# Padding the k features to full weight loads, masking kv by a factor, and one queue for the first loads, in a fused attention and feed-forward kernel

## The chip, the cores and the metric

The kernel runs on one core of a Trainium2 chip. A core has five engines that run their own instruction streams and wait for each other by semaphores: TensorE (PE, with its weight loads shown apart as PEld), VectorE (DVE), ScalarE (ACT), GpSimd (POOL) and SyncE (SP), which here only issues DMA transfers. ACT and POOL can issue transfers too; each issuing engine has a queue of its own. The metric is the device time of one execution in microseconds. Lower is better.

## The reference

One block on an input of 2048 tokens by 448 features (bf16): a layer norm, then linear attention with 16 heads of 28 features whose feature map is a pair of softmaxes, and beside it a feed-forward part; both are added to the input.

```python
xn = layernorm(x)
# attention
q, k, v = split_heads(xn @ wqkv)                    # 16 heads of 28
pq, pk  = q @ w_phi, k @ w_phi                      # per head, 28 x 28
phi     = lambda p: concat(softmax(p), softmax(-p)) # 56 features per head
kv  = einsum("bhsf,bhsd->bhfd", phi(pk), v)
z   = einsum("bhsf->bhf", phi(pk))
num = einsum("bhqf,bhfd->bhqd", phi(pq), kv)
den = einsum("bhqf,bhf->bhq", phi(pq), z)[..., None] + 1e-6
A   = merge_heads(num / den) @ wo
# feed-forward
B   = silu(xn @ w1) @ w2                            # 448 -> 1792 -> 448
out = x + A + B
```

## The kernel before

Tokens are cut into 16 tiles of 128, each tile a set of rows on the 128 partitions. Nearly every matmul works on 64 contraction rows, and two of them, on the low and the high half of the rows, run side by side.

**Stages.** Each tile is normalised on DVE (`ln_tile`: statistics `bnst`, `bnag`; scale `rstd`; result `xn`). Tiles 0 to 3 are turned over by TensorE (`tr0` to `tr3`) and evicted from PSUM (`ev0` to `ev3`); tiles 4 to 15 are turned over by transposing transfers in SP's queue (`xnT_dma`). The weights of q and k are folded with w_phi in the kernel (`fold_k`, `fold_q`, words f and g of the plan below), from weights that are transposed by transfers (`wT_dma`). The feed-forward's first half is cut into 28 blocks of 256 hidden columns by 512 tokens (words F0 to F27), each evicted by ACT as a silu. v, k and q are made for pairs of tiles (words v, k, q). A k or q block is evicted by ACT as two exponentials, exp(p) and exp(-p), into a tile `Ek_sb` or `Ek_hi`; DVE makes 32 sums and reciprocals; POOL multiplies (`phik` for k in place, `phiq` for q into RA). For q, a transposing transfer in SP's queue (`phqT`) then puts the product into phT.

**kv.** Word K takes two tiles. For each tile, the 896 features (16 heads of 56) are cut into 8 chunks of 112 (two heads). A chunk's features are the weights and two heads' v, with a column of ones, the 58 moving columns; low and high rows go into two PSUM banks, 7 and 6. For the first seven chunks, 128 weight columns are loaded instead of 112: 16 columns of the next chunk go with them, and what they produce is not read. The last chunk has nothing behind it in the tile and loads 112 (`wide`). After the last K, word M (`kvm`) adds the two banks and keeps of each chunk the two diagonal blocks, one per head, by a product with a 0/1 mask: the result is KVm.

**U, W and the rest.** Word U multiplies phT by KVm for a pair of tiles, 8 chunks each; DVE divides (`den`, `rden`, `o`), a transposing transfer in SP's queue turns the result over (`oT_dma`), and word W multiplies it by wo. Words G, Y and E are the second half of the feed-forward; DVE adds the result to x (`out_ev`) and a store follows. A word with a leading a is the first half of its block, with b the second, on the other row halves; "@" names the PSUM banks.

**What sets the order.** Transfers at the start are issued in the order of the code: x tiles 0, 1, 2 to 3, then w1 columns 0 to 511 in two parts (`w1_0`, `w1_0r`) in SP's queue; w1 columns 512 to 1023 (`w1_512`) in ACT's queue, behind a first activation `warm_act`; then the rest of w1, wv, x and others by SP. While these come in, TensorE runs 38 warm-up matmuls. The first three F blocks are then done tile by tile of 128 tokens, in an order written out in a list (00a is block 0, tile 0, first two of three weight row blocks; 00b the third). Chains of names fix the order of the first instructions on DVE and ACT. After that TensorE follows PLAN, a list of 184 words. On the other engines a list scheduler puts the instructions in order, from a model of durations, latencies and transfer rates written in the code; the order of TensorE is fixed by PLAN, and the model's numbers alone change no computation.

**Places.** `kv` (word K), `kvm` (word M), `ek` and `eq` (the k and q feature tiles; q reuses the tiles of `Ek_sb` in a ring of 8), `load`, `load_x` and `load_w1` (first loads), `ones_column` (sets the last feature of each group to one), `phi_q` and `slot` (where tiles of q go in phT: `Ek_hi` and w1 lie in phT's space, so some slots come free with the last K, others with the last F). All matmuls of the program are recorded at one line, L508; ACT's activations at L531; POOL's fills at L538; ordinary loads at L545; transposing transfers at L613.

Of the kernel before, what the change touches and what calls it, by code (L numbers as in the profile page):

```python
# [140 lines left out]
class _Prog:  # L141
# [86 lines left out]
    def schedule(self, stalls=()):  # L228
# [53 lines left out]
        while done < n:  # L282
# [77 lines left out]
          ("pool", "pe"): 100.0}  # L360
PLAN = """r0 aF3@4 r2 r1 bF3 aF6@0 aF4@6 bF6 bF4 aF5@4 av2@2 av0@0 bv2 bF5 av4@6 bv0 bv4 aF10@2 aF9@0 bF10 f0@6 bF9 aF12@4 aF7@2
aF11@0 f1@6 bF11 bF7 bF12 aF25@0 ak2@6 bF25 bk2 av8@4 av12@2 bv8 ak0@0 bv12 bk0 av10@6 aF22@4 bv10 aF17@2 bF22 av14@6
aF14@0 bF17 bv14 aF18@4 bF14 aF27@6 ak4@2 bF27 bF18 bk4 av6@6 ak6@0 ak8@4 bv6 bk8 bk6 ak12@2 aF8@6 bk12 bF8 aY0@45
aF21@0 aY0 aF23@2 bF21 bF23 ak14@6 bY0 g0@1 bk14 bY0 aF13@0 aF19@2 bF13 aF20@4 bF19 aF24@6 bF20 bF24 ak10@0 g1@3 bk10 K0
K6 K4 aq4@2 K12 aq8@4 bq4 K8 K2 s4 aq0@0 bq8 aq6@2 K14 bq0 bq6 bY1@45 K10 M aY1 aq2@2 aF26@0 s6 bq2 bY1 bF26 aG3@23 aY1
aU2@67 s8 aF15@0 bU2 s0 bF15 aF16@4 bG3 bF16 aU4@01 aq12@6 bU4 bq12 aU3@45 bG3 bU3 s2 aG3 aq10@0 aq14@6 bq10 s10 aW2@45
bq14 aG2 aU0@01 bG2 aG4@67 bU0 bW4 bG2 bW2 s12 bG4 aG2 s14 aW3 aG4 aU1@01 bW3 aW4 bU1 bG4 bG5@23 aU5@50 aG6@41 aU6@67
bU5 aG5 bG6 aU7@05 bU6 bG5 bG6 aG5 bU7 aG6 aW0@67 bW5 bW0 aW5 aW6 aW1@05 bW6 bW7@672 bW1 aW7 E14 E15"""


def bass_parallel_sum__linear_kernel_hedgehog__dense_activation_silu__prompt_kernel(
# [36 lines left out]
    with es:  # L408
        def sb(name, shape, dt):
            return es.enter_context(nc.sbuf_tensor(name, shape, dt))  # L410
# [30 lines left out]
        w1_sb = flat[:, 0:4 * FF].rearrange("p (k f) -> p k f", k=4)  # L441
        NEK = 8
        EW = 2 * D
        Ek_sb = sb("Ek_sb", [128, NEK, EW], BF16)
        Ek_hi = flat[:, 4 * FF:4 * FF + NEK * EW].rearrange("p (n c) -> p n c", n=NEK)

# [357 lines left out]
        def proj_block(t, b0, is_k):  # L804
# [3 lines left out]
            def evac():  # L808
                E2 = ek(t, 2)[:, :, 0:2 * D] if is_k else eq(t, 2)
# [60 lines left out]
        def kvm():  # L870
            lo, hi = (banks[KVB - i][0:KP, 0:2 * DA * CC] for i in range(2))
            P.op("act", d_act(464), lambda e: e.activation(kvsum[:], hi, ACTF.Identity), reads=[hi], writes=[kvsum[:]], name="kvhi")
            P.op("dve", d_dve(464), lambda e: e.tensor_tensor(kvsum[:], lo, kvsum[:], ALU.add), reads=[lo, kvsum[:]], writes=[kvsum[:]], name="kvsum")
            src = kvsum[:].rearrange("p (c j e) -> p c j e", c=CC, j=2)
# [205 lines left out]
        for word in PLAN.split():  # L1080
# [159 lines left out]
```

## Time and profile before

| | |
|---|---|
| runs shown, us | 165.96, 148.22, 146.32 (median 148.22) |
| profiled execution, us | 146.37 |
| its span, first to last instruction, us | 145.1 |
| granted TensorE clock, mean | 1.000 |
| busy, share of span | PE 98%, DVE 62%, ACT 55%, POOL 52% |
| DVE's largest groups | sums of k and q features, 24.4 us in 20 instructions |
| POOL's largest groups | products of q features 27.1 us, of k features 26.8 us |
| ACT table loads | 11, 14.1 us |

How to read the profile: times are microseconds unless marked ns. A row of groups reads: line of the code, engine, operation, output tile, input tile, shapes, count, then busy time, mean ns of one, and the idle time of the engine just before them with what ended it. A row of the timeline reads: start, length, engine, line, operation, count. A row of the chain reads: start, length, what. Tiles that share memory are shown under the name of the memory: w1 and the high k tiles as phT, the q features as Ek_sb, normalised tiles and phiq as RA, transposed weights as Y_sb. Matmuls are pipelined, so their ends are modelled; the step from one start to the next is what counts.

### The profile page before, as it was taken

How to read it: one execution, taken by the hardware profiler on the slowest of the kernel's cores; microseconds unless marked ns; L12 is line 12 of the kernel's file. 1: busy time of each engine (PE TensorE's matmuls, PEld its weight loads, DVE VectorE, ACT ScalarE, POOL GpSimd, SP SyncE). 2: the span in 40 equal slices, each digit the busy share in tenths (PEclk: the TensorE clock that was granted, in tenths of full speed). 3: DMA queues.
4: the chain of work that ended last, by engine and by line, in shares of the span. 5: the costliest groups of instructions: out<-in, count | busy, mean ns of one | idle time of the engine just before them, and what ended most of it. 6: DMA issues, size and time to landing. Idle time of an engine off the chain costs nothing.

```text
span 145.1 us, 4509 instructions
## 1 busy us (share of the span) xinstructions
PE 141.6 (98%) x1947; PEld 83.6 (58%) x1947; DVE 89.5 (62%) x195; ACT 79.4 (55%) x96; POOL 75.1 (52%) x93
## 2 busy tenths in 40 slices
PE   7999999999999999999999999999999999999994
PEld 7895444445444544476787655565555555555663
DVE  1969898600760069939049999927796384625822
ACT  4567856479995999979887949228620000000000
POOL 8808567620197008799935999991497600000000
PEclk9999999999999999999999999999999999999999
DMA  4999998746970000000000069959889999633432
GB/s 101 347 346 266 283 153 119 147 87 139 356 203 5 0 2 5 0 0 5 0 5 5 0 88 195 124 108 181 76 164 164 214 193 167 134 74 72 133 127 63
DMA packets 44500, 17.59 MB, mean 121 GB/s; under 512 B 37040, under 2 KB 44096, under 8 KB 44480
## 3 DMA queue, kind: packets, MB, share of 16 engines
q1 hardware_dynamic: 41648, 15.10, 52.7%
q10 hardware_dynamic: 2704, 2.17, 5.3%
q8 instruction: 15, 0.25, 0.8%
q14 instruction: 5, 0.04, 0.1%
q0 software_dynamic: 128, 0.03, 0.1%
HBM read 6.57 MB, written 1.84 MB: 58 GB/s over the span
## 4 chain that ended last, share of the span: by engine, by line
PE 93%; DMA 3%; SPq 1%; DVE 0%; issue 0%
PE psum L508 93%; DMA phT<-in_B_w_dram 3%; SPq L545 1%; PE psum L525 0%; DVE x_sb L988 0%
## 5 line engine op out<-in xcount | busy, mean ns | idle before, releaser
L508 PE MATMUL psum<-xnT,phT 64*128 64x512 bf16 (+1 forms) x428 | 46.9, 350 | 0.3 <-ACT xnT L531 0.2
L508 PE MATMUL psum<-w_sb,hT 64*128 64x448 bf16 (+2 forms) x434 | 46.1, 343 | 0.0
L825 DVE TENSOR_REDUCE Rec<-Ek_sb 128x32 f32<-128x896 bf16 (+1 forms) x20 | 24.4, 1251 | 19.0 <-ACT Ek_sb L531 19.0
L531 ACT ACTIVATE hT<-psum 128x1024 bf16<-128x1024 f32 x28 | 27.7, 1023 | 11.2 <-PE psum L508 11.0
L508 PEld LDWEIGHTS psum<-xnT,phT 64*128 64x128 bf16 (+1 forms) x428 | 22.5, 95 | 18.5 <-ACT vaug L531 0.6
L508 PEld LDWEIGHTS psum<-w_sb,hT 64*128 64x128 bf16 (+1 forms) x434 | 23.2, 94 | 17.2 <-issue 0.2
L861 POOL TENSOR_TENSOR RA<-Ek_sb,Rec 128x896 bf16<-128x896 bf16 x16 | 27.1, 1724 | 6.1 <-DVE Rec L826 5.0
L508 PE MATMUL psum<-Wqk,xnT 64*128 64x432 bf16 x224 | 24.4, 343 | 0.0
L531 ACT ACTIVATE Ek_sb<-psum 128x864 bf16<-128x864 f32 x24 | 20.3, 915 | 5.9 <-PE psum L508 3.7
L835 POOL TENSOR_TENSOR Ek_sb<-Ek_sb,Rec 128x896 bf16<-128x896 bf16 x8 | 13.4, 1699 | 17.7 <-DVE Rec L826 17.6
L508 PEld LDWEIGHTS psum<-Wqk,xnT 64*128 64x128 bf16 x224 | 11.2, 95 | 8.1
L531 ACT ACT_TABLE_LOAD x11 | 14.1, 1283 | 1.7 <-PEq L1225 0.8
L835 POOL TENSOR_TENSOR phT<-phT,Rec 128x896 bf16<-128x896 bf16 x8 | 13.4, 1699 | 1.2 <-issue 0.9
L988 DVE TENSOR_TENSOR x_sb<-psum,x_sb 128x448 bf16<-128x448 f32 (+1 forms) x13 | 7.2, 584 | 9.1 <-PE psum L508 9.1
L508 PE MATMUL psum<-wv,xnT 64*128 64x448 bf16 x112 | 12.2, 349 | 0.0
L690 DVE BATCH_NORM_STATS2 st<-x_sb 128x6 f32<-128x448 bf16 x16 | 9.6, 603 | 2.9 <-DMA x_sb<-in_A_x_dram 2.9
L508 PE MATMUL psum<-wo_sb,vaug 64*128 64x448 bf16 (+1 forms) x102 | 10.7, 338 | 0.0
L705 DVE TENSOR_SCALAR RA<-x_sb,mv,rstd 128x384 bf16<-128x384 bf16 (+4 forms) x29 | 9.0, 348 | 1.6 <-POOL rstd L701 1.5
L967 DVE TENSOR_TENSOR vaug<-psum,rden 128x448 bf16<-128x448 f32 x16 | 9.2, 619 | 0.0
L825 DVE TENSOR_REDUCE Rec<-phT 128x64 f32<-128x1792 bf16 x4 | 8.0, 1990 | 1.9 <-ACT phT L531 1.9
L826 DVE RECIPROCAL Rec<-Rec 128x32 f32<-128x32 f32 (+1 forms) x24 | 8.8, 396 | 0.2
L508 PEld LDWEIGHTS psum<-wv,xnT 64*128 64x128 bf16 x112 | 5.3, 94 | 5.6 <-ACT vaug L531 0.5
(60 smaller groups left out, 109.7 us busy)
## 6 DMA issues: line engine op xcount, KB each, us to landing
out_dram<-x_sb ACTq DMA_DIRECT2D x15, 112.0 KB, 2.4
w_sb<-in_B_w_dram SPq DMA_DIRECT2D x1, 1568.0 KB, 7.9
x_sb<-in_A_x_dram SPq DMA_DIRECT2D x3, 448.0 KB, 6.0
wo_sb<-in_A_wo_dram SPq DMA_DIRECT2D x2, 336.0 KB, 7.5
phT<-in_B_w_dram SPq DMA_DIRECT2D x1, 576.0 KB, 7.0
phT<-in_B_w_dram SPq DMA_DIRECT2D x2, 256.0 KB, 4.4
phT<-in_B_w_dram ACTq DMA_DIRECT2D x1, 384.0 KB, 4.6
wv<-in_A_wqkv_dram SPq DMA_DIRECT2D x1, 336.0 KB, 7.2
```

The costliest lines, as they stand in the source:

```text
L508: r = e.matmul(dst, lhsT, rhs, start=st, stop=sp, skip_group_check=True)
L531: P.op("act", d_act(n), lambda e: e.activation(dst, src, func, scale=scale), reads=[src], writes=[dst], table=table, name=name, **keys)
L545: P.dma(lambda e: e.dma_start(out=dst, in_=src), n / 280.0, writes=[dst], name=name, eng=eng, lat=lat)
L690: P.op("dve", 590, lambda e: e.bn_stats(st6[:, t, :], xs), reads=[xs], writes=[st6[:, t, :]], name=f"bnst{t}", okeys_w=["ln"])
L705: P.op("dve", dur, lambda e: e.tensor_scalar(dst, x_sb[:, t, c0:c1], mv[:, t, 0:1], rstd[:, t:t + 1], ALU.subtract, ALU.mult), reads=[xs, ...
L825: P.op("dve", 50 + 967 * n, lambda e: e.tensor_reduce(R2, E4, AXL.X, ALU.add), reads=[E4], writes=[R2], name="Ssum")
L826: P.op("dve", 135 + 210 * n, lambda e: e.reciprocal(R2, R2), reads=[R2], writes=[R2], name="Rrec")
L835: P.op("pool", 1700, lambda e: e.tensor_tensor(E3, E3, Rk[:, :, None].broadcast_to([128, 32, DH]), ALU.mult), reads=[E3, Rk], writes=[E3], ...
L861: P.op("pool", 1700, lambda e: e.tensor_tensor(dst, Eq, Rq.rearrange("p (c j) -> p c j", c=CC)[:, :, :, None].broadcast_to([128, CC, 4, DH ...
L967: P.op("dve", 620, lambda e: e.tensor_tensor(o3, U3[:, :, 0:DH], rden[:, uq, :, None].broadcast_to([128, H, DH]), ALU.mult), reads=[U3[:, ...
L988: P.op("dve", d_dve(cs.stop - cs.start), lambda e: e.tensor_tensor(res[:, cs], ob, addend[:, cs], ALU.add), reads=[ob, addend[:, cs]], wri ...
```

## The change

Four things are changed. (1) Each k tile gets 16 columns of zeros behind its 896 features (EW = 2*D + 16), filled once by POOL, so that the last chunk loads 128 weight columns too. Ten tiles instead of eight lie in `Ek_sb`, six in `Ek_hi`; the ring of q stays at eight (NEQ). kvsum gives up its own memory and takes that of wv. (2) `kvm` masks by a factor per partition: two ACT copies with a scale, and two DVE instructions that multiply by the factor and add. (3) All first loads go by SP's queue, w1_0 ahead of x tiles 2 and 3, and w1_512 behind w1_0r; blocks 0 and 1 take all three weight row blocks of a tile at once; tile 3's `bnag` goes behind tile 2's `xn` on DVE. (4) PLAN is a new order of the same 184 words, and some numbers of the model differ.

```diff
-PLAN = """r0 aF3@4 r2 r1 bF3 aF6@0 aF4@6 bF6 bF4 aF5@4 av2@2 av0@0 bv2 bF5 av4@6 bv0 bv4 aF10@2 aF9@0 bF10 f0@6 bF9 aF12@4 aF7@2
-aF11@0 f1@6 bF11 bF7 bF12 aF25@0 ak2@6 bF25 bk2 av8@4 av12@2 bv8 ak0@0 bv12 bk0 av10@6 aF22@4 bv10 aF17@2 bF22 av14@6
-aF14@0 bF17 bv14 aF18@4 bF14 aF27@6 ak4@2 bF27 bF18 bk4 av6@6 ak6@0 ak8@4 bv6 bk8 bk6 ak12@2 aF8@6 bk12 bF8 aY0@45
-aF21@0 aY0 aF23@2 bF21 bF23 ak14@6 bY0 g0@1 bk14 bY0 aF13@0 aF19@2 bF13 aF20@4 bF19 aF24@6 bF20 bF24 ak10@0 g1@3 bk10 K0
-K6 K4 aq4@2 K12 aq8@4 bq4 K8 K2 s4 aq0@0 bq8 aq6@2 K14 bq0 bq6 bY1@45 K10 M aY1 aq2@2 aF26@0 s6 bq2 bY1 bF26 aG3@23 aY1
-aU2@67 s8 aF15@0 bU2 s0 bF15 aF16@4 bG3 bF16 aU4@01 aq12@6 bU4 bq12 aU3@45 bG3 bU3 s2 aG3 aq10@0 aq14@6 bq10 s10 aW2@45
-bq14 aG2 aU0@01 bG2 aG4@67 bU0 bW4 bG2 bW2 s12 bG4 aG2 s14 aW3 aG4 aU1@01 bW3 aW4 bU1 bG4 bG5@23 aU5@50 aG6@41 aU6@67
-bU5 aG5 bG6 aU7@05 bU6 bG5 bG6 aG5 bU7 aG6 aW0@67 bW5 bW0 aW5 aW6 aW1@05 bW6 bW7@672 bW1 aW7 E14 E15"""
+PLAN = """r2 aF3@4 r0 r1 bF3 aF4@6 aF6@0 bF4 bF6 aF5@4 av2@2 av0@6 bv2 bF5 bv0 av4@2 aF8@0 bv4 f0@6 aF9@4 bF8 bF9 aF12@2 aF10@6
+f1@0 aF11@4 bF10 bF11 bF12 aF7@0 aF27@6 bF7 ak4@2 av10@4 bF27 av6@0 bv10 bv6 bk4 av8@4 av14@6 ak6@0 bv14 bv8 bk6 aF23@2
+aF21@6 aF20@4 bF23 aF14@0 bF21 bF20 bF14 aF18@2 ak0@6 bF18 bk0 av12@0 ak8@4 bv12 ak10@2 bk8 bk10 ak2@6 aF13@0 bk2 bF13
+bY0@45 aF17@2 bY0 bF17 ak12@6 aY0 g1@1 bk12 aY0 aF26@0 aF16@2 bF26 bF16 aF19@4 aF24@6 bF19 bF24 ak14@0 g0@2 bk14 K0 K10
+K2 K6 aq4@4 aq8@2 bq4 K4 aq6@0 K12 bq6 s4 bq8 aY1@45 K8 aY1 aq0@2 K14 aq2@0 bq0 bY1 M bY1 s6 bq2 aF22@2 aF25@6 bF22 bF25
+aU2@45 aF15@0 bU2 bF15 aG3@23 s8 s0 aq12@6 aq10@0 aU3@45 bq10 bU3 bG3 bG3 bq12 aG2@45 aU4@01 bG2 aq14@6 aG2 aW2 bU4 s2
+bW2 s10 bG2 bq14 s12 aG4@01 aW3 bG4 aU0@56 bW3 aU5@47 bU0 aG3 bW4 bG4 bU5 aU1@62 aG6@53 bU1 aG6 aG4 bG6 bG5@47 aU6@26
+aW4 bG5 bU6 s14 aG5 aU7@01 aG5 bU7 bG6 bW1@26 bW5 aW1 aW5 bW0@01 aW6 aW0 aW7@264 bW6 bW7 E14 E15"""
...
-        NEK = 8
-        EW = 2 * D
+        NEK, NEQ = 10, 8
+        EW = 2 * D + 16
...
-        kvsum = sb("kvsum", [KP, CC * 2 * DA], F32)
+        kvsum = wv[0:KP, 0:4 * DA * CC].bitcast(F32)
...
         load_x(0, 1)
         load_x(1, 2)
+        load(w1_sb[:, 0:2, 0:512], B_w1[0:256, 0:512].rearrange("(k p) f -> p k f", p=128), "w1_0")
         load_x(2, 4)
-        load(w1_sb[:, 0:2, 0:512], B_w1[0:256, 0:512].rearrange("(k p) f -> p k f", p=128), "w1_0")
...
-        load_w1(512, 1024, "act")
+        load_w1(512, 1024)
...
-            def wide(c):
-                return slice(0, 128) if c < CC - 1 else slice(0, KP)
-
...
-            pe_mms([(banks[KVB - i][wide(c), c * 2 * DA:(c + 1) * 2 * DA], ek(t)[r, 0, c * KP:c * KP + wide(c).stop],
+            pe_mms([(banks[KVB - i][:, c * 2 * DA:(c + 1) * 2 * DA], ek(t)[r, 0, c * KP:c * KP + 128],
...
-            P.op("act", d_act(464), lambda e: e.activation(kvsum[:], hi, ACTF.Identity), ...)
-            P.op("dve", d_dve(464), lambda e: e.tensor_tensor(kvsum[:], lo, kvsum[:], ALU.add), ...)
-            P.op("dve", d_dve(464), lambda e: e.tensor_tensor(
-                KVm[0:KP], src, mask2[:, None, :, None].broadcast_to([KP, CC, 2, DA]), ALU.mult), ...)
+            for j in range(2):
+                P.op("act", d_act(232), lambda e, j=j: e.activation(src[:, :, j, :], hi[:, :, j, :], ACTF.Identity, scale=mask2[:, j:j + 1]), ...)
+            for j in range(2):
+                P.op("dve", d_dve(232), lambda e, j=j: e.scalar_tensor_tensor(
+                    KVm[0:KP, :, j, :], lo[:, :, j, :], mask2[:, j:j + 1], src[:, :, j, :], ALU.mult, ALU.add), ...)
...
-        chain("bnst0 bnag0 bnst1 bnag1 rstd0 xn0a xn0 rstd1 xn1 bnst2 bnag2 bnst3 bnag3 rstd2 xn2 rstd3 xn3 ev3".split())
-        chain("warm_act w1_512 ve0 ve1 ev0a ev0 ev1 ve2 ve3 ev2 silu_table".split())
-        byname = {o.name: o for o in P.ops}
-        byname["w1_512"].deps.add(byname["warm_act"].id)
-        byname["w1_512"].odeps -= byname["w1_512"].deps
+        chain("bnst0 bnag0 bnst1 bnag1 rstd0 xn0a xn0 rstd1 xn1 bnst2 bnag2 bnst3 rstd2 xn2 bnag3 rstd3 xn3 ev3".split())
+        chain("warm_act ve0 ve1 ev0a ev0 ev1 ve2 ve3 ev2 silu_table".split())
...
-        for word in "tr0a tr0 tr1 00a 10a 01a 11a 00b 10b 01b 11b tr2 20 21 tr3 02 12 22 03 13 23".split():
+        for word in "tr0a tr0 tr1 00 10 01 11 tr2 20 21 tr3 02 12 22 03 13 23".split():
...
-        chain(["vaug1", "kvm0", "wphi", "wphi1", "wphi2", "wphi3"])
+        memset(Ek_sb[:, :, 2 * D:EW], 0.0, 128, "pad0")
+        memset(Ek_hi[:, :, 2 * D:EW], 0.0, 128, "pad1")
+        chain(["vaug1", "kvm0", "wphi", "wphi1", "wphi2", "wphi3", "pad0", "pad1"])
```

More of the change, by code (lines that the diff above doesn't have):

```diff
@@ L441, in bass_parallel_sum__linear_kernel_hedgehog__dense_activation_silu__prompt_kernel @@
         w1_sb = flat[:, 0:4 * FF].rearrange("p (k f) -> p k f", k=4)
-        NEK = 8
-        EW = 2 * D
+        NEK, NEQ = 10, 8
+        EW = 2 * D + 16
         Ek_sb = sb("Ek_sb", [128, NEK, EW], BF16)
-        Ek_hi = flat[:, 4 * FF:4 * FF + NEK * EW].rearrange("p (n c) -> p n c", n=NEK)
+        Ek_hi = flat[:, 4 * FF:4 * FF + (NT - NEK) * EW].rearrange("p (n c) -> p n c", n=NT - NEK)
         def ek(t, w=1):
@@ L538, in memset, with load @@
             P.op(eng, d_pool(n, 0.5), lambda e: e.memset(dst, v), writes=[dst], name=name)
-        def load(dst, src, name, eng="sp", lat=1700.0):
+        def load(dst, src, name, eng="sp", lat=1900.0):
             n = 2
@@ L544, in load @@
                 n *= cnt
-            P.dma(lambda e: e.dma_start(out=dst, in_=src), n / 280.0, writes=[dst], name=name, eng=eng, lat=lat)
+            P.dma(lambda e: e.dma_start(out=dst, in_=src), n / 290.0, writes=[dst], name=name, eng=eng, lat=lat)
         memset(ones_bf[:], 1.0, 128, "ones")
@@ L580, in load_x @@
         def load_x(t0, t1):
-            load(x_sb[:, t0:t1, :], rows_of(A_x, t0, t1), f"x{t0}", lat=1400.0)
+            load(x_sb[:, t0:t1, :], rows_of(A_x, t0, t1), f"x{t0}", lat=1250.0 if t0 < 2 else 1500.0)
         def load_rows4(dst, src, c0, c1, name, eng="sp"):
@@ L790, in eq @@
         def eq(t, w=1):
-            n = q_order.index(t) % NEK
+            n = q_order.index(t) % NEQ
             return Ek_sb[:, n:n + w, :]
@@ L808, in evac @@
             def evac():
-                E2 = ek(t, 2)[:, :, 0:2 * D] if is_k else eq(t, 2)
+                E2 = ek(t, 2)[:, :, 0:2 * D] if is_k else eq(t, 2)[:, :, 0:2 * D]
                 src = psum[:, b0 * 512:(b0 + 2) * 512].rearrange("p (i c) -> p i c", i=2)[:, :, 0:DQ].rearrange("p i (h f) -> p i h f", f=DF)
@@ L840, in kv @@
         def kv(ts):
-            def wide(c):
-                return slice(0, 128) if c < CC - 1 else slice(0, KP)
             P.cur_slack = 250.0
-            pe_mms([(banks[KVB - i][wide(c), c * 2 * DA:(c + 1) * 2 * DA], ek(t)[r, 0, c * KP:c * KP + wide(c).stop],
+            pe_mms([(banks[KVB - i][:, c * 2 * DA:(c + 1) * 2 * DA], ek(t)[r, 0, c * KP:c * KP + 128],
                      vaug[r, t, 2 * c:2 * c + 2, :].rearrange("p h c -> p (h c)"),
                      t == 0 and c == 0, t == NT - 1) for t in ts for c in range(CC) for i, r in enumerate((LOW, HIGH))],
-                   "kv_mm", dur=CC * 31.2 * len(ts), keys_w=["kvbank"], mode=64)
+                   "kv_mm", dur=CC * 28.7 * len(ts), keys_w=["kvbank"], mode=64)
             P.cur_slack = 0.0
@@ L857, in phi_q @@
             sp = n % NPQ
-            Eq = eq(t)[:, 0, :].rearrange("p (c j f) -> p c j f", c=CC, f=DH)
+            Eq = eq(t)[:, 0, 0:2 * D].rearrange("p (c j f) -> p c j f", c=CC, f=DH)
             dst = phq[:, sp, :, 0:KP].rearrange("p c (j f) -> p c j f", f=DH)
@@ L870, in kvm @@
         def kvm():
[L871 to L874, printed above, removed]
-            P.op("dve", d_dve(464), lambda e: e.tensor_tensor(
-                KVm[0:KP], src, mask2[:, None, :, None].broadcast_to([KP, CC, 2, DA]), ALU.mult),
-                reads=[src, mask2[:]], writes=[KVm[0:KP]], name="kvm")
+            lo, hi = (banks[KVB - i][0:KP, 0:2 * DA * CC].rearrange("p (c j e) -> p c j e", c=CC, j=2) for i in range(2))
+            src = kvsum.rearrange("p (c j e) -> p c j e", c=CC, j=2)
+            for j in range(2):
+                P.op("act", d_act(232), lambda e, j=j: e.activation(src[:, :, j, :], hi[:, :, j, :], ACTF.Identity, scale=mask2[:, j:j + 1]),
+                     reads=[hi, mask2[:]], writes=[src[:, :, j, :]], name="kvhi")
+            for j in range(2):
+                P.op("dve", d_dve(232), lambda e, j=j: e.scalar_tensor_tensor(
+                    KVm[0:KP, :, j, :], lo[:, :, j, :], mask2[:, j:j + 1], src[:, :, j, :], ALU.mult, ALU.add),
+                    reads=[lo, src, mask2[:]], writes=[KVm[0:KP, :, j, :]], name="kvm")
         early = {int(w[2]) for w in PLAN.split() if w[1:2] == "Y"}
@@ L1124, in bass_parallel_sum__linear_kernel_hedgehog__dense_activation_silu__prompt_kernel @@
                 kv(range(t0, t0 + 2))
-                if t0 < NEK:
+                if t0 < NEQ:
                     ones_column(t0, t0 + 2)
```

## The prediction

> **What bounds the kernel now.** I read the page first, then the chain of work that ended last, then TensorE's own timeline, because all three turn out to say the same thing. From the page:
>
> ```profile
> span 145.1 us, 4509 instructions
> ...
> PE 141.6 (98%) x1947; PEld 83.6 (58%) x1947; DVE 89.5 (62%) x195; ACT 79.4 (55%) x96; POOL 75.1 (52%) x93
> ...
> PEclk9999999999999999999999999999999999999999
> ```
>
> TensorE is busy for 98% of the span and its granted clock is full in every slice. The chain, in order of time, shows where the other 2% lies:
>
> ```profile
> 2.68 5.04 DMA phT<-in_B_w_dram
> ...
> 9.50 30.98 PE psum L508 x345
> ...
> 40.48 102.59 PE psum L508 x1503
> ...
> 143.10 0.39 DVE x_sb L988
> ```
>
> Two unbroken runs of matmuls hold 9.50 to 143.07 us. Ahead of them stands one transfer of w1; behind them one DVE addition and the last store. A busy TensorE can hide slow matmuls, so I compared matmul starts in the timeline: blocks of 64-row matmuls of 512, 448 and 432 columns start every 108, 94.5 and 91.2 ns, 0.211 ns a column in all three. They scale with their columns alone, so no fixed cost is left in them. By that rate 16 matmuls of 58 columns would take 196 ns; over it lie 0.05 us in each kv tile and 0.03 in each U tile, and in all the rest a few stops of 0.05 to 0.2 us. A change of order alone can therefore gain a few tenths at most after 11.44 us; it can lose much more.
>
> **Part 1: kv weight loads.** For each of 16 tiles, kv issues 16 matmuls of 58 columns; 14 load 128 weight columns, the two of the last chunk only 112. Two groups by form (last columns: busy us, mean ns, idle before):
>
> ```profile
> L508 PEld LDWEIGHTS psum<-vaug,Ek_sb 64*128 64x128 bf16 x112 | 2.2, 97 | 0.1
> ...
> L508 PEld LDWEIGHTS psum<-vaug,Ek_sb 64*112 64x112 bf16 x16 | 1.1, 127 | 0.0
> ```
>
> The narrower load is the longer one. What that costs is read from TensorE's timeline (start, us, count), where the same 58-column matmul also occurs with 128-column loads only, in U:
>
> ```profile
> 72.58 1.67 PE L508 MATMUL psum<-vaug,Ek_sb 64*128 64x58 bf16 x96
> 74.08 0.72 PE L508 MATMUL psum<-Wqk,xnT 64*128 64x432 bf16 x6
> ```
>
> ```profile
> 121.75 0.62 PE L508 MATMUL psum<-KVm,phT 64*128 64x58 bf16 x32
> 122.20 2.81 PE L508 MATMUL psum<-w_sb,hT 64*128 64x448 bf16 x28
> ```
>
> From start to next start, 96 kv matmuls take 1.50 us (250 ns a tile) and 32 U matmuls 0.45 (225 to 229 ns a tile). 16 tiles by 22 ns are **0.36 us off TensorE**, on the path, since no other engine releases these blocks later than TensorE reaches them. Bounds: 0 (a load is hidden by something else) to 0.40 (225 ns everywhere). The 16 padding columns cost two POOL fills behind the four small loads of w_phi; POOL is idle there from 6.73 to 10.61 us waiting for those loads, and a 128x128 fill took 0.2 us: nothing, and 0.4 us of BD's start if that cover went.
>
> The Trainium skill, "TensorE: Matmul & The Clock Gate", section "LDWEIGHTS (loading the stationary operand)", puts a load at its columns divided by 1.2 ns: 93 ns for 112 columns, 107 for 128. By that the padding would make 32 loads 13 ns longer, an estimate of 0.4 us lost instead of 0.36 won. The trace differs (127 against 97 ns), and the measurement decides.
>
> **Part 2: the kv mask.** Before, one ACT copy (0.57 us), one DVE sum (0.58) and one DVE product with the mask (0.85) make KVm. After, two half-width ACT copies with a factor and two half-width DVE multiply-adds. No row shows the new DVE form; between half the sum's row (0.29) and half the product's (0.43) each, I take 0.4, so DVE falls from 1.43 to about 0.8 us and ACT rises from 0.57 to about 0.7. KVm was ready at 90.44 us, U began at 91.10, so this has 0.66 us of cover and is worth nothing at that U; one engine up and one down, it changes no sum. kvsum in wv's space waits for the last v block, 30 us earlier.
>
> **Part 3: the start.** TensorE's timeline:
>
> ```profile
> 6.11 0.69 PE L508 MATMUL psum<-xnT,phT 128*128 128x128 bf16 x8
> 7.00 1.38 PE L508 MATMUL psum<-xnT,phT 128*128 128x128 bf16 x16 [0.20 <-ACT xnT L531]
> 8.22 0.39 PE L525 MATMUL psum<-ident,RA 128*128 128x128 bf16 x4
> 8.44 0.83 PE L508 MATMUL psum<-xnT,phT 128*128 128x128 bf16 x12
> 9.11 0.39 PE L525 MATMUL psum<-ident,RA 128*128 128x128 bf16 x4
> 9.33 2.93 PE L508 MATMUL psum<-xnT,phT 128*128 128x128 bf16 x42
> ```
>
> Eight matmuls run on w1's first two row blocks; eight more wait for tile 1 (7.00); the last eight of these 24 wait for w1_0r, which landed at 7.71 (2.68 + 5.04, the chain). In the change the 24 are no longer split, so the third matmul already needs w1_0r. Its landing: before it in SP's queue stand x0, x1, w1_0 and x2 (704 KB) as before, but w1_512 (384 KB) no longer comes beside it in ACT's queue. Between x2's landing (1.74 + 2.7 = 4.4) and that of w1_512r (8.1), 1024 KB landed: 278 KB/us. From x1's landing at 3.35, w1_0, x2 and w1_0r (736 KB) give 6.0 us, x2 about 5.1 (DVE takes it at 5.57), w1_512 about 7.4. Then: 12 matmuls at 55.8 ns from 6.2 end by 6.9; 12 more from 7.0 by 7.67; tile 2's transposes wait for its normalisation, which ends at 7.77, so 7.87 instead of 8.22. The change puts tile 3's statistics behind that normalisation; its chain (bnag3 0.18, square root 0.3, reciprocal 0.15, normalisation 0.4, with their hand-overs) ends at about 8.9 instead of 8.27, so its transposes go at about 8.95 and the stretch at 9.33 begins at 9.15: **-0.2 us**. Bounds: -0.45 (tile 3 not late) to +0.8 (w1_0r lands as before, a rival below). SP issues one load more (0.43 us) ahead of x4 and all behind it; those landings are set by bytes (x4 6.0 us, wv 7.2, x8 8.4 after issue, where x0 took 2.1), so nothing, and up to 0.4 us if x8 or the transposes come later.
>
> **Part 4: the order.** I laid the 184 words of both plans end to end with the durations of TensorE's rows (half blocks: F 0.65 and 0.86 us, v 0.57 and 0.76, k and q 0.55 and 0.73, G and Y 1.32, U 0.23, W 0.76 and 0.57, K 0.50 before and 0.46 after). The words are the same; for the old plan the sum ends at 142.3 against 143.07, so I add the difference to both. Then I looked where a word comes nearer to what it needs. The nearest is in the fold of Wqk: f0 moves from 24.3 to 22.8, and its banks are reused by F10 at 25.9 (25.7 with part 3), where before f1 took them at 27.29. DVE's timeline:
>
> ```profile
> 23.99 0.59 DVE L705 TENSOR_SCALAR RA<-x_sb,mv,rstd 128x384 bf16<-128x384 bf16 x2
> 25.17 0.60 DVE L705 TENSOR_SCALAR RA<-x_sb,mv,rstd 128x384 bf16<-128x384 bf16 x2 [0.59 <-POOL rstd L701]
> 25.69 1.12 DVE L683 TENSOR_TENSOR Wqk<-psum,last_k 128x432 bf16<-128x432 f32 x2
> ```
>
> The two subtractions that free the banks stood behind tile 15's normalisation, to 26.82. One fits into the 0.59 us gap before it; the other would end at 26.3, which with its hand-over stops F10 for 0.8 us. If both go ahead, nothing stops. I take **+0.2**, nearer to nothing, because before the same reuse (26.82 for 27.29) waited for nothing. Elsewhere: F27 needs tile 15's transpose, landed at 29.59, at 30.3; K14 comes at 82.4 for a k block done at 72.1, as K10 did before (82.1 for 72.2); U3 at 94.9 for tiles landed by 91.7; F20 at 42.1 and F13 at 54.0 follow ACT's evictions of v8 and v12 within 0.1 us. These cost nothing by my sum, and 0.1 to 0.4 each if it is off.
>
> **Sum.** The profiled execution took 146.37 us, 1.27 over its span. 146.37 - 0.36 - 0.2 + 0.2 = **146.0 us**. The median of the runs shown is 148.22, the fastest 146.32: the profiled run stands with the fastest, and my sum is for such runs; a median raised in the same way would be near 147.9.
>
> **The rivals.** (1) w1_0r comes no earlier. The skill's "DMA: Bandwidth & Descriptors", "Issuing engines are not separate DMA queues", says that issuing from several engines saves only issue time; by that the landing stays at 7.71. For it: the same bytes share the engines. Against: they would no longer share them before w1_0r. Price: 22 matmuls from 7.76 end at 8.99, transposes 9.21, 12 matmuls 9.88, transposes 10.1 instead of 9.33: +0.77 in place of -0.2, **147.0**. (2) The tight places of part 4 open: F10's 0.8 us and two or three of the evictions at 0.2 to 0.4 each, with part 1 kept: **147.2**. For it: f0's DVE work has no room; against: the waits shown now sum to tenths. (3) Slower: U5 moves from 119.7 to 112.0, but its transposed tiles 10 and 11 landed at 113.0 (issued 107.35, 5.6 us), behind the pair 2, 3 in SP's queue, which is served in order. q10 is also early (its matmuls end at 95.9, not 102.1); ACT, the sums and two POOL products of 1.72 us give an issue at 104 and a landing at 109.6, in time. It decides at whether the pair goes into the queue ahead of U4's two output transposes (ready at about 106 and 107, 1.3 us each): behind them it is issued at 109.7, lands at 115.4, and TensorE stands for 3.6 us: **149.6**, slower than before by over 2%. (4) Padding does not shorten the loads: 146.4 at most with part 3 as summed, 146.8 by the page's formula.
>
> **How the numbers follow.** Forecast 62% (145.3 to 146.6: part 1 and the bounds of part 3 below, part 4's 0.8 above); rival 1 12%; rival 2 14% (up to 148.0); rival 3 5%; rival 4 3%; better than 145.3 4%. The range 145.3 to 148.0 leaves out rival 3, the last case and some of rival 2. A measurement of this kernel tells about 2% from no change, 2.9 us: faster than 143.4 is out of reach of any sum here and needs a lowered comparison (3%); slower than 149.3 is rival 3 and a raised run (6%); within, 91%.
>
> **What will show it.** Right: kv loads all near 94 ns and 228 ns a tile; the 12 matmuls at 6.1 us without a gap over 0.2; the long matmul stretch starting near 9.15; no stop at F10 near 26 us, nor before U5 near 112. Wrong: w1_0r landing after 6.6, TensorE idle for over 1 us between 11 and 143 us, or KVm later than 90 us.

## The result and the profile after

The changed kernel takes **149.01 us** (median of 20 executions, 147.67 to 150.77), the kernel before 146.97 (20, 146.28 to 165.96) beside it: a ratio of **1.0123**, 95% interval 1.0098 to 1.0147. (The ratios here and below leave out disturbed executions; the medians hold all.) That is within the 2% that count as no change, but the loss is there, and it lies outside the forecast range of 145.3 to 148.0 and on its wrong side. The kernel before had medians of 146.55, 146.58, 147.25 and 146.71 us in the four sets of experiments, so ratios of different sets are compared with an uncertainty of some 0.3%; kernels of one set are compared directly.

The profiled execution took 148.91 us with a span of 147.7: 2.54 us above before's 146.37. Its page:

```profile
span 147.7 us, 4516 instructions
...
PE 141.2 (96%) x1947; PEld 84.5 (57%) x1947; DVE 89.2 (60%) x195; ACT 79.6 (54%) x97; POOL 74.7 (51%) x95
...
PEclk9999999999999999999999999999999999999999
```

TensorE has as many matmuls as before and 0.4 us less work; the span grew because it stands. Where it does is told by its waits (line waited for: us in total, times, longest):

```profile
PE psum L508 <- DVE Wqk L683: 1.1, 1, 1.1
PE psum L508 <- DMA vaug<-vaug: 1.1, 1, 1.1
...
PE psum L508 <- ACT ve L694: 0.8, 1, 0.8
PE psum L508 <- DMA phT<-in_B_w_dram: 0.3, 1, 0.3
```

Of these four the profile of before has none; its TensorE, once begun, had one wait of 0.2 us in this view. The first two break the long run of matmuls, as the chain of work that ended last shows in order of time:

```profile
5.16 6.53 DMA Wp<-in_A_w_phi_dram
11.75 0.10 issue
11.86 0.56 POOL BD L620
12.41 0.23 POOL BD L624
12.65 0.23 POOL ve L699
12.95 0.58 POOL rstd L701
13.56 0.60 DVE RA L705 x2
...
27.19 0.53 DVE Wqk L683
27.72 0.14 issue
27.86 105.54 PE psum L508 x1557
...
133.50 4.45 DMA vaug<-vaug
137.95 0.14 issue
138.09 7.53 PE psum L508 x62
```

Before, the chain went from one transfer of w1 into TensorE at 7.76 us and stayed there to the last matmul. Now it begins with a load of w_phi, goes through POOL and the layer norm on DVE, and enters TensorE at 27.86; and near the end a transposing transfer breaks it once more. Each part by its size, from TensorE's timeline (step from start to start against the step of an unbroken block):

| where | us against before |
|---|---|
| start: the first 64-row matmul of 512 columns at 12.03 instead of 11.44 | +0.59 |
| stop at F10, 26.37 to 27.86 | +1.27 |
| a stop of 0.16 at 40.1 before, gone | -0.16 |
| kv, 16 tiles | -0.36 |
| stop in W7, 136.64 to 138.09 | +1.26 |
| sum (the span: +2.54) | +2.60 |

**The start.** TensorE's timeline (start, length, count; in brackets the idle time ahead and what ended it):

```profile
5.99 0.28 PE L508 MATMUL psum<-xnT,phT 128*128 128x128 bf16 x2
7.12 1.39 PE L508 MATMUL psum<-xnT,phT 128*128 128x128 bf16 x22 [0.84 <-ACT ve L694]
8.34 0.39 PE L525 MATMUL psum<-ident,RA 128*128 128x128 bf16 x4
8.56 0.44 PE L508 MATMUL psum<-xnT,phT 128*128 128x128 bf16 x5
9.30 0.56 PE L508 MATMUL psum<-xnT,phT 128*128 128x128 bf16 x7 [0.29 <-DMA phT<-in_B_w_dram]
9.70 0.39 PE L525 MATMUL psum<-ident,RA 128*128 128x128 bf16 x4
9.92 3.36 PE L508 MATMUL psum<-xnT,phT 128*128 128x128 bf16 x46
```

Two matmuls run, then TensorE waits for the third row block: w1_0r landed at 6.98. (The row names an ACT instruction that began at 6.80, `ve`; what it makes is no input of these matmuls.) The second stop, at 8.8, waits for w1_512's third row block, landed at 9.25. The stretch that the forecast put at 9.15, and that began at 9.33 before, begins at 9.92.

**kv.** The groups by form hold no load of 112 columns any more (last columns: busy us, mean ns, idle before):

```profile
L508 PEld LDWEIGHTS psum<-vaug,Ek_sb 64*128 64x128 bf16 x160 | 2.9, 94 | 0.4
...
L508 PEld LDWEIGHTS psum<-vaug,phT 64*128 64x128 bf16 x96 | 1.8, 94 | 0.3
```

and in TensorE's timeline

```profile
75.16 1.08 PE L508 MATMUL psum<-vaug,Ek_sb 64*128 64x58 bf16 x64
76.07 1.27 PE L508 MATMUL psum<-Wqk,xnT 64*128 64x432 bf16 x12
```

64 matmuls take 0.91 us from start to next start, 228 ns a tile instead of 250.

### The profile page after: what moved, and what is told of

Same layout as the page of the kernel before. It is cut to its first block, busy times and chain, and to the rows that moved or that the text cites. A ratio compares the mean times of both kernels' runs of the same rounds, so it can differ in the third digit from the quotient of the medians.

```text
span 147.7 us, 4516 instructions
## 1 busy us (share of the span) xinstructions
PE 141.2 (96%) x1947; PEld 84.5 (57%) x1947; DVE 89.2 (60%) x195; ACT 79.6 (54%) x97; POOL 74.7 (51%) x95
## 4 chain that ended last, share of the span: by engine, by line
PE 77%; DVE 9%; DMA 7%; POOL 5%; issue 1%; POOLq 0%; DVEq 0%; SPq 0%
PE psum L508 77%; DMA Wp<-in_A_w_phi_dram 4%; DVE RA L705 4%; DVE st L690 3%; DMA vaug<-vaug 3%; POOL Wp L545 1%; POOL rstd L701 1%; POOL vaug L538 1%; DVE mv L691 1%; DVE Wqk L683 1%; POOL BD L620 0%; POOL ve L699 0%; POOL KVm L538 0%; DVE x_sb L986 0%; POOL ident L548 0%
## 5 line engine op out<-in xcount | busy, mean ns | idle before, releaser
L508 PE MATMUL psum<-xnT,phT 64*128 64x512 bf16 (+1 forms) x428 | 46.1, 350 | 2.2 <-DVE Wqk L683 1.1
L825 DVE TENSOR_REDUCE Rec<-Ek_sb 128x32 f32<-128x896 bf16 (+1 forms) x21 | 26.4, 1289 | 23.1 <-ACT Ek_sb L531 23.0
L508 PEld LDWEIGHTS psum<-xnT,phT 64*128 64x128 bf16 (+1 forms) x428 | 23.2, 95 | 20.0 <-ACT hT L531 1.6
L531 ACT ACTIVATE hT<-psum 128x1024 bf16<-128x1024 f32 x28 | 27.1, 1024 | 7.2 <-PE psum L508 7.1
L858 POOL TENSOR_TENSOR RA<-Ek_sb,Rec 128x896 bf16<-128x896 bf16 x16 | 26.6, 1701 | 8.3 <-DVE Rec L826 8.3
L531 ACT ACTIVATE Ek_sb<-psum 128x864 bf16<-128x864 f32 x26 | 22.2, 919 | 11.3 <-DVE x_sb L986 7.2
L835 POOL TENSOR_TENSOR Ek_sb<-Ek_sb,Rec 128x896 bf16<-128x896 bf16 x10 | 16.7, 1698 | 20.9 <-DVE Rec L826 20.9
L835 POOL TENSOR_TENSOR phT<-phT,Rec 128x896 bf16<-128x896 bf16 x6 | 10.1, 1700 | 1.0 <-DVE Rec L826 1.0
L508 PEld LDWEIGHTS psum<-wv,xnT 64*128 64x128 bf16 x112 | 5.9, 94 | 4.8
L531 ACT ACTIVATE vaug<-psum 128x896 bf16<-128x896 f32 x8 | 7.1, 922 | 2.7 <-PE psum L508 2.7
```

The lines of the kernel that those rows point to most:

```text
L508: r = e.matmul(dst, lhsT, rhs, start=st, stop=sp, skip_group_check=True)
L531: P.op("act", d_act(n), lambda e: e.activation(dst, src, func, scale=scale), reads=[src], writes=[dst], table=table, name=name, **keys)
L825: P.op("dve", 50 + 967 * n, lambda e: e.tensor_reduce(R2, E4, AXL.X, ALU.add), reads=[E4], writes=[R2], name="Ssum")
L835: P.op("pool", 1700, lambda e: e.tensor_tensor(E3, E3, Rk[:, :, None].broadcast_to([128, 32, DH]), ALU.mult), reads=[E3, Rk], writes=[E3], ...
L858: P.op("pool", 1700, lambda e: e.tensor_tensor(dst, Eq, Rq.rearrange("p (c j) -> p c j", c=CC)[:, :, :, None].broadcast_to([128, CC, 4, DH ...
```

## The experiments

The questions: does part 1 give what the trace says; what in the start costs, the queue, the uncut list or both; is the stop at F10 a matter of the order or of late loads; and what holds the last transposed tiles.

**Parts 1 and 2 alone (e1).** The kernel before with the padding, the full loads, kvsum in wv's space and the new mask; its own start, PLAN and model numbers.

```diff
-        NEK = 8
-        EW = 2 * D
+        NEK, NEQ = 10, 8
+        EW = 2 * D + 16
...
+        memset(Ek_sb[:, :, 2 * D:EW], 0.0, 128, "pad0")
+        memset(Ek_hi[:, :, 2 * D:EW], 0.0, 128, "pad1")
```

> The kernel before with parts 1 and 2 alone (padded k rows, mask by a factor); its loads, its start and its order stay. Theory T (the loss of the change lies in three stops of TensorE: at the start, at F10 and in W7; the padding itself is worth what it was summed at): 0.36 us under the kernel before, some 146.0 against 146.4, ratio 0.9975; a kv tile takes 228 ns. Rival P (the padding or the new mask costs something that the profile of the change hides, as the 10 tiles of Ek_sb or a later KVm): 146.4 or more.

146.52 us beside 146.55, ratio 0.9983 (0.9954 to 1.0013). 228 ns a tile here too. The 0.36 us are in the rows; in the time they can't be told from nothing. What the expectation didn't have is a stop of 0.82 us in W at 134.9: the old order has one there as well, in an execution where the last transposed tiles took 4.03 us to land instead of 2.46.

**Parts 1, 2 and 4 (e5).** The same with the new PLAN, and before's start.

```diff
-PLAN = """r0 aF3@4 r2 r1 bF3 ...
+PLAN = """r2 aF3@4 r0 r1 bF3 ...
```

> The changed kernel without part 3: the new order, the padding and the mask, but the loads, the split of blocks 0 and 1 and the chains of before. Theory T (the stop at F10 is mostly due to a LayerNorm that is 1.3 us late behind the slower loads): the long stretch of matmuls starts at 9.3 to 9.4 us, F10 stops for 0.3 to 0.7 us instead of 1.3, W7 for 0.5 to 1.2; granted clock 1.0 throughout; some 147.0, ratio 1.0035. Rival O (the order puts F10 too early whatever the loads do): the stop at F10 is over 1.0 us, 147.7 or more.

147.34 us beside 146.58, ratio 1.0039 (1.0017 to 1.0061). The stop at F10 is there with before's start too, but it is 0.49 us and not 1.27; the one in W7 is 0.61.

**The start alone (e2).** The changed kernel with before's PLAN; its own start, parts 1 and 2 and its model numbers stay.

```diff
-PLAN = """r2 aF3@4 r0 r1 bF3 ...
+PLAN = """r0 aF3@4 r2 r1 bF3 ...
```

> The changed kernel with the plan of before: parts 1, 2 and 3, not 4. Theory T: the long stretch of matmuls starts 0.6 us late as in the changed kernel; the LayerNorm of tiles 4 to 15 is about 1.2 us late behind the loads of w_phi; the old order has more room there, so f1 and F25 stop for 0.3 to 0.5 us together; no stop in W7. 146.4 - 0.36 + 0.6 + 0.4 = 147.0, ratio 1.005. Rival O (the order alone is at fault, and the loads cost only their 0.6 at the start): 146.6, no stop between 11 and 32 us.

147.66 us beside 146.55, ratio 1.0067 (1.0032 to 1.0101); e1, of the same set, is 1.14 us faster and differs by the start and the scheduler's numbers. And here the profile shows what that of the changed kernel did not. The page's row of the granted clock:

```profile
PEclk9959999999999999999999999999999999999999
```

and the stretches of the timeline (stretch: length, TensorE busy, matmuls, granted clock, DMA share, GB/s):

```profile
4.31:7.72 3.41, 1.55 (x22) 1.00 0.96 250
7.72:11.13 3.41, 3.41 (x34) 0.50 1.01 355
11.13:14.54 3.41, 3.41 (x55) 1.00 1.33 338
```

For 3.41 us the clock is granted at half, right behind 3.41 us in which TensorE was busy for 1.55, since it waited 1.65 us for w1_0r (landed at 7.51). In that second window matmuls of 128 columns start every 107 ns instead of every 56. The mean clock of such an execution is 0.988, and each execution lists its own, so they can be counted: below 0.995 in 10 of 20 of the changed kernel and in 5 of 12 here, against 2 of 102 of the kernel before in the four sets. Full-clock executions of e2 have a median of 147.40, the others 148.42. The stops at f1 and F25 that the expectation priced are not in this profile, whose TensorE came late to them because of the clock.

**w1_512 in ACT's queue (e3).** The changed kernel, with the one load back where it was.

```diff
-        load_w1(512, 1024)
+        load_w1(512, 1024, "act")
...
-        chain("warm_act ve0 ve1 ...
+        chain("warm_act w1_512 ve0 ve1 ...
```

> The changed kernel with one load moved back: w1 columns 512 to 1023 in ACT's queue, behind the first activation. Theory T (one queue moves the first bytes more slowly than two, and w_phi's small loads land later for it): the last of the loads that BD waits for lands by 10.8 us instead of 11.7, the stop at F10 falls from 1.3 to 0.3 us or less, the stop for w1_512r at 9.3 us goes: 1.4 to 1.6 us under the changed kernel, some 147.4, ratio 1.007. Rival B (the same bytes take the same time whoever issues them): landings within 0.3 us of the changed kernel's, 148.5 or more.

147.51 us, ratio 1.0052 (1.0018 to 1.0087), in the set of e2. The list is still uncut, the stop at 6.0 us is 1.36, and the clock drops in 5 of 12. At full clock the median is 147.09; that of the changed kernel is 148.47.

**Constant matmuls in the stop (e6).** 16 matmuls on constants, whose result is not read, behind the first two of block 0: they fill most of the stop and save no wait.

```diff
+            if word == "00":
+                for i in range(16):
+                    o = P.op("pe", 0.0, lambda e: e.matmul(banks[3][:, 0:128], ones_bf[:], ones_bf[:], start=True, stop=True), ...)
```

> The changed kernel with 16 matmuls on constants (some 0.9 us) put where TensorE stands still for w1_0r, after the second matmul of block 0; they write to a bank that is not yet in use and nothing reads them. Theory C (the stop of 1.0 to 1.6 us at 6 us is what lets the granted clock fall to half for 3.4 us in about half of the executions): granted clock 1.0 in all or nearly all executions, the median 0.4 to 0.7 us under the changed kernel's, the single executions no lower than its best (147.7). Rival N (the clock falls for something else): 0.988 in a third or more of the executions, the median unchanged.

148.29 us beside 146.58, ratio 1.0089 (1.0055 to 1.0124), with the clock full in all 6. Its timeline:

```profile
5.88 0.28 PE L508 MATMUL psum<-xnT,phT 128*128 128x128 bf16 x2
5.99 1.06 PE L1028 MATMUL psum<-ones_bf 128*128 128x128 bf16 x16
7.48 1.39 PE L508 MATMUL psum<-xnT,phT 128*128 128x128 bf16 x22 [0.43 <-DMA phT<-in_B_w_dram]
```

So it is the standing, and not the uncut list as such, that the lower clock goes with, as far as six executions tell it: at the rate of the kernels that stand (24 of 60, below), none in six would come by chance one time in twenty. And the rest of the loss is no matter of the clock, because with a full clock it is still 0.9%.

**The cut list (e9), and the cut list with two queues (e10).** The changed kernel with before's list for the first blocks; e10 also has w1_512 in ACT's queue, as in e3.

```diff
-        for word in "tr0a tr0 tr1 00 10 01 11 tr2 ...
+        for word in "tr0a tr0 tr1 00a 10a 01a 11a 00b 10b 01b 11b tr2 ...
```

> After, with only the first list cut as before: blocks 0 and 1 of tiles 0 and 1 take w1's first two row blocks (00a 10a 01a 11a) and then the third (00b ...); all first loads stay in SP's queue. Theory D, the start costs in two separate ways, the standing TensorE near 6 us (through the granted clock) and the late landings of one queue: the matmuls at 6 us run without a stop over 0.4 us, no execution has a mean clock below 0.995, but w1_512r still lands after 9.0 us, w_phi after 11.5, and F10 near 26 us still stops 0.7 to 1.3 us; ratio to the kernel before 1.007 to 1.009, between the 1.0123 of after and the 1.0039 of the kernel with the old start. Rival S, the cut list is all of it: ratio 1.004, as with the old start. Rival Q, the cut is nothing and only the queue counts: 1.0123 and clocks below 0.995 in some executions.

> After, with the first list cut as before and w1_512 in ACT's queue again; w1_0 ahead of x tiles 2 and 3, and tile 3's bnag behind tile 2's xn, stay as in after. Theory D: both costs of the start are gone, so ratio 1.004 (147.2 us beside 146.6), as with the whole old start (1.0039), no execution with a clock below 0.995, w_phi landed by 11.5 us. Rival X, that the x tiles 2 and 3 behind w1_0 cost by themselves: 1.006 or more, tile 2's transposes after 8.3 us in the profile.

e9: 148.67 us beside 147.25, ratio 1.0083 (1.0050 to 1.0115). e10, in the same set: **147.06**, ratio **0.9985** (0.9959 to 1.0010). No execution of either lost clock (0 of 12 each). With the list cut in both, moving one load from SP's queue to ACT's is worth 1.6 us: both costs are there, and the queue is the larger. Two timelines, e9:

```profile
7.95 0.62 PE L508 MATMUL psum<-xnT,phT 128*128 128x128 bf16 x8 [0.53 <-DMA phT<-in_B_w_dram]
8.40 0.39 PE L525 MATMUL psum<-ident,RA 128*128 128x128 bf16 x4
9.02 0.99 PE L508 MATMUL psum<-xnT,phT 128*128 128x128 bf16 x12 [0.23 <-DMA phT<-in_B_w_dram]
```

and e10:

```profile
7.26 1.07 PE L508 MATMUL psum<-xnT,phT 128*128 128x128 bf16 x16 [0.24 <-ACT xnT L531]
8.16 0.39 PE L525 MATMUL psum<-ident,RA 128*128 128x128 bf16 x4
8.39 0.83 PE L508 MATMUL psum<-xnT,phT 128*128 128x128 bf16 x12
```

e9 waits twice for w1, e10 for none of it. The landings (and BD, POOL's product of w_phi, which reads the first three of its four loads):

| us | before | after | e9 | e10 |
|---|---|---|---|---|
| w1_0r landed | 7.71 | 6.98 | 7.90 | 7.58 |
| third row block of w1_512 landed | 8.10 | 9.25 | 9.39 | 7.92 |
| x tiles 4 to 7 landed | 9.69 | 10.45 | 10.79 | 9.85 |
| third w_phi load landed | 10.44 | 11.68 | 11.31 | 11.01 |
| last w_phi load landed | 11.01 | 11.87 | 11.58 | 11.33 |
| BD begins | 10.61 | 11.86 | 11.48 | 11.18 |
| first matmul of 512 columns | 11.44 | 12.03 | 12.17 | 11.46 |

(The other two row blocks of w1_512 landed at 8.97 in e9, which is what its wait at 9.02 ended with.) BD begins 0.17 to 0.18 us behind the third w_phi load in all four. Its row before and after, with POOL's idle time ahead of it:

```profile
10.61 0.56 POOL L620 TENSOR_TENSOR BD<-Wp,mask_half 128x224 bf16<-128x224 bf16 x1 [3.88 <-DMA Wp<-in_A_w_phi_dram]
...
11.86 0.56 POOL L620 TENSOR_TENSOR BD<-Wp,mask_half 128x224 bf16<-128x224 bf16 x1 [4.94 <-DMA Wp<-in_A_w_phi_dram]
```

e10 was expected at 1.004, as e5 with the whole old start, and came out 0.5% below it; the two are of different sets, and what part of that is real stays open. The kernel before had its highest median, 147.25, in e10's set; against its 146.55 to 146.71 in the others e10's 147.06 would be a loss of 0.35 to 0.5 us. Only e9 against e10 is free of this.

**BD later on POOL (e4).** BD waits for w_phi and stands ahead of tile 4's scale in POOL's queue. Here the two BD products go behind tile 7's rstd.

```diff
         chain("ev3 bnst4".split())
+        chain("rstd7 bdphi bd0".split())
```

> The changed kernel, but on POOL the two products that make BD from w_phi stand behind the scale of tile 7 instead of ahead of that of tile 4; no load is moved. Theory T (POOL's queue stands still behind w_phi, and with it every normalisation from tile 4 on): tile 4's scale at 11.5 to 12.3 us instead of 13.5, tiles 12 to 15 done 1.0 to 1.2 us earlier, the stop at F10 0.3 us or less, 1.0 us under the changed kernel, some 147.9, ratio 1.010. Rival X (the normalisation is late because x tiles 4 to 7 land at 10.45 instead of 9.69): the stop stays over 0.8 us, 148.5 or more.

148.08 us beside 146.55, ratio 1.0101 (1.0048 to 1.0154). rstd4 came at 11.83 and tile 4's normalisation at 12.57, 1.0 us earlier than in the changed kernel, as meant, and F10 stopped for 0.19 instead of 1.27. But F10 went on at 27.77, hardly sooner than at 27.86. In this profile x tiles 8 to 11 landed at 16.85 (in the others at 14.93 to 15.78), the statistics of tile 8 could not begin before 16.88, and tile 15's normalisation came at 26.50 instead of 26.59. TensorE came to F10 later because it had stopped for 0.83 us at 23.31 for transposed weights (Y_sb), whose transfers stand behind that load in SP's queue. At full clock the median is 147.81, that of the changed kernel 148.47: a gain of 0.7 us at most, over two sets. So BD holds up tile 4 on POOL, as the 1.0 us shows; what that is worth at F10 this profile doesn't show, because another wait took its place.

**The last W words.** Four kernels exchange words near the end, so that the block that reads the last transposed tiles comes later. e7, in the changed kernel:

```diff
-... aW7@264 bW6 bW7 E14 E15
+... bW6 aW7@264 bW7 E14 E15
```

> The changed kernel with the last half of W6 ahead of the first half of W7, so that W7 is called 0.57 us later; all other engines keep their order. Theory W (W7 waits for the last output transpose, which lands late because the DMA engines stand still around an instruction fetch, at a time that the order of TensorE does not move): the landing stays near 138, the stop in W7 falls from 1.3 by about 0.5 us, 0.3 to 0.5 us under the changed kernel. Rival V (that transpose follows TensorE, so its landing moves with the order): the stop stays as it is, no gain.

148.15 us beside 146.58, ratio 1.0090 (1.0063 to 1.0116). The stops in W7 fell from 1.26 to 0.10 and 0.22 us. At full clock 148.04, where the changed kernel has 148.47: a gain of some 0.4 us that is as large as the sets differ.

e8, in e1, whose order has the same place:

```diff
-... aW1@05 bW6 bW7@672 bW1 aW7 E14 E15
+... aW1@05 bW6 bW1 bW7@672 aW7 E14 E15
```

> The kernel before with parts 1 and 2 and, in the old order, the last half of W1 ahead of the second half of W7, so that W7 is called 0.57 us later. Theory W: the stop of 0.8 us that the profile of the padded kernel with the old order shows in W7 at 134.9 us falls below 0.3; 0.2 to 0.4 us under that kernel, some 146.0 to 146.2 where the kernel before has 146.5, ratio 0.997. Rival V: no difference from it, ratio 0.998 to 1.0.

146.56 us beside 146.58, ratio 0.9997 (0.9974 to 1.0020). The stops are 0.20 and 0.24 instead of 0.82; no gain that can be measured.

e11 is e10 with the exchange of e7; e12 has, besides, f1's matmuls ahead of F10's first half.

```diff
-... aF12@2 aF10@6 f1@0 aF11@4 ...
+... aF12@2 f1@0 aF10@6 aF11@4 ...
```

> After with the cut first list and w1_512 in ACT's queue (as in e10), and the second half of W6 ahead of the first half of W7. Theory W: the wait for W7's transposed tiles shrinks from 1.02 + 0.11 us (profile of e10) to 0.2 to 0.4, worth 0.6 us in such a profile and 0.3 to 0.6 in the median: ratio to the kernel before 0.995 (146.0 to 146.4 us beside 146.6). Rival V, as the same exchange in the old order gave no measurable gain, the end is set by the transfer itself: 0.9985, with a stop left before the last block.

> As e11, and f1's matmuls (0.27 us, banks 0 and 1) ahead of F10's first half, whose banks 6 and 7 wait for the fold's subtractions. Theory F: the stop of 0.49 us at F10 falls to about 0.2, f1's own banks being free by then: 0.2 to 0.3 us less than e11, ratio 0.993 to 0.994. Rival: F8's second silu has not freed bank 0 or 1 when f1 comes, f1 stops for 0.2 to 0.4 us in F10's place: as e11.

e11: 146.73 us beside 146.71, ratio 0.9991 (0.9966 to 1.0017). e12, same set: 146.44, ratio 0.9989 (0.9962 to 1.0016). In the profile of e12 F10's stop, now behind f1, falls from the 0.49 us of e10 to 0.26 (26.00 to 26.28), as expected; the last stop is 0.22 us; its span of 144.9 us is, with e8's, the shortest of all. In e11's profile F10 doesn't stop, but TensorE had stopped for 0.50 us at 22.71 for transposed weights. Yet neither beats the kernel before by what this measurement can tell, and neither reached its expectation of 0.995 and 0.993. The two words exchanged at the end are not shown to be worth anything.

## Why the prediction was wrong, step by step

**Part 1 was right in its size**: loads at 94 ns, 250 to 228 ns a tile, 0.36 us off TensorE. Rival 4 did not occur, and the padding fills at 6.43 and 6.73 us on POOL lay where the forecast put them, in idle time. In the end-to-end time 0.2% is what e1 shows, with an interval that holds nothing and all of it.

**Part 2 was right.** The two new DVE instructions took 0.36 and 0.45 us (estimate 0.4 each), the two ACT copies 0.45 and 0.46; KVm was done before 88 us and U began at 92.6. No stop came of it.

**Part 3 is the step that failed**, in three of its terms.
- *The rate.* I put w1_0r's landing at 6.0 by 278 KB/us, a rate read where SP's and ACT's queues both had loads. With one queue, 736 KB from x1's landing (3.38) to w1_0r's (6.98) came at 204 KB/us; and x1 to x4, the same 1696 KB in both kernels, took 7.07 us instead of 6.34, that is 240 against 267 KB/us. I had reasoned that the same bytes no longer share the engines; but the engines moved less, 304 GB/s from 3.4 to 9.4 us against 344 before (e9 308, e10 342). And 6.98 is an early one: in the five other profiles with one queue w1_0r landed at 7.31 to 7.90, in the eight with two at 7.29 to 7.85. Rival 1, that it comes no earlier than 7.71, was nearer to this than my 6.0; its price left out the next item.
- *What comes behind w1_0r.* "Those landings are set by bytes, so nothing": w1_512's third block landed at 9.25 instead of 8.10 and stopped block 2; the third w_phi load came 1.24 us later. POOL's wait for w_phi was in before's profile at 3.9 us, and I used it only as cover for the padding. I did not follow the instructions queued behind it: BD, then tile 4's scale, so that a late w_phi makes the layer norm late from tile 4 on, up to the place where another wait ends later (in e4, x tiles 8 to 11). e10, which undoes the queue and the list and nothing else, is not slower than the kernel before in its set; e9 against e10 gives the queue 1.6 us.
- *The clock.* Cutting the list less leaves TensorE standing for 1.0 to 1.65 us, and in part of the executions the granted clock then falls. Over all kernels run: below 0.995 in 24 of 60 executions with the uncut list and the stop, in 0 of 6 with the stop filled, in 1 of 84 with the cut list. The changed kernel's median is 149.23 in executions with the lower clock and 148.47 at full clock. No term of the sum had this.

**Part 4: the mechanism was right, the size was not.** DVE's timeline after the change:

```profile
25.91 0.60 DVE L683 TENSOR_TENSOR Wqk<-psum,last_k 128x432 bf16<-128x432 f32 x1
26.59 0.60 DVE L705 TENSOR_SCALAR RA<-x_sb,mv,rstd 128x384 bf16<-128x384 bf16 x2
27.11 0.60 DVE L683 TENSOR_TENSOR Wqk<-psum,last_k 128x432 bf16<-128x432 f32 x1
```

One subtraction went ahead of tile 15's normalisation and one behind it, the case that the forecast priced at 0.8 us before it took 0.2. But tile 15's normalisation had moved from 25.17 to 26.59, because of part 3, so the stop was 1.27. With before's start it was 0.49 (e5) and so it was in e10: between the two values. The other profiles with one queue, the new order and a full clock have 0.87 (e6), 0.73 (e7) and 0.76 (e9), so 1.27 is a large one. The new order seems to pay more for late loads than the old one (e2 against e1, old order: 1.0 us at full clock; e9 against e10, new order: 1.6). The other tight places stayed closed as summed; rival 3 did not occur, tiles 10 and 11 were issued at 107.17 and landed at 111.49.

**What no step had: the last transposed tiles.** The forecast has no term for them; in before's profile the last two such transfers landed after 2.43 and 2.46 us. Their landing in the changed kernel, 4.45 us, is not due to the new order alone: e1 and e8 have 4.03 and 3.98 with the old one. The last section tells what goes with it. But all ten profiles with the new order have such a landing, and only two of the four with the old one; so the part of the 2.54 us that this stop makes (1.26) can be a difference of two profiled executions as well as of two kernels. As an estimate, the medians' loss of 2.0 us can be put together without it: the queue's 1.4 to 1.6 us (with the stop at F10 that comes of it), some 0.5 us of clock, a few tenths of the order, less 0.2 to 0.36 of kv.

What stays open: whether the new order costs anything at a good start (e10 says no, e5 says 0.2 to 0.6%), whether it makes the late landing at the end more frequent, and why one queue moves less than two.

## What to carry to other kernels

Take a transfer rate only from rows with the same number of queues at work; before a load is moved, go through every in-order queue for the first instruction that waits for it or for a load behind it, and count what stands behind that instruction. Where TensorE must stand at the start, cut the work so that part of it can run meanwhile: the stop costs its length, and the clock may take as much again. And compare a profile's stop with other executions before it is put down to the change: one of the two largest here was in the old order as well.

## What the hardware showed that was not expected

**A window that is half busy can be followed by a lower clock.** In e2 and e3 a window of 3.41 us in which TensorE was busy for 1.55 and 1.85 us was followed by 3.41 us at half clock; in the changed kernel's profile the window from 5.71 to 9.12, with 2.44 us busy, was followed by none. In the profiles that show where windows begin, these lie differently against the program (at 4.31 us in e2, 5.71 in the changed kernel), which fits that some executions were hit and others not. The Trainium skill, "TensorE: Matmul & The Clock Gate", section "Part 1: The HAM clock gate (the "warmup" mystery)", states a free-running window of about 3.4 us, which agrees, and a fall after a whole idle one, which these rows go beyond: 45 to 54% busy was not enough to keep the clock.

**Two queues move these first loads sooner than one.** From x1's landing to that of x tiles 4 to 7, the same 1696 KB took 6.85 to 7.51 us in the six profiles with one queue and 5.83 to 6.74 in the eight with two, 1.6 us in the end (e9, e10). "DMA: Bandwidth & Descriptors", "Issuing engines are not separate DMA queues", in the Trainium skill states that several issuing engines save only the time to issue. The issues themselves were 0.43 to 0.5 us each and ran well ahead of the landings here, so for these loads the measurement differs.

**Where a transposing transfer meets an instruction transfer, it lands late.** In 12 of 14 profiles a 16 KB transfer of instructions (0.9 to 1.6 us) began 1.07 to 1.96 us after the last transposing transfer was issued, that is before it could land; in these it landed after 3.71 to 4.45 us. In the two others, the kernel before and e2, no such transfer fell into it (135.61 and 138.56 us, after the landings at 134.64 and 136.52), and it took 2.46 and 2.42 us. Of the last six transposing transfers of each profile, 84 in all, the 40 into which a 16 KB transfer of instructions fell took 3.09 to 4.49 us, and the other 44 (in one of them it began 0.06 us before the landing) 2.41 to 2.50. In the changed kernel, almost nothing else was done moving between 135.5 and 136.5 us: packets of 0.9 and 2.2 KB in the two halves. This is a coincidence seen in every profile; no run moved the one transfer to see the other follow.
